# Masked attention and gated MLP on one core: who scales the first batch's probabilities, and when a table is cleared

## The chip, the cores and the metric

The kernel runs on one core of a Trainium2 chip, in one launch. The metric is device time in microseconds (us) of a whole execution. The engines of the core are named as the profile names them: PE (TensorE, matmuls; its weight loads are listed apart as PEld), DVE (VectorE), ACT (ScalarE), POOL (GpSimd) and SP (SyncE, whose queue issues all the DMAs of this kernel).

## The reference

Attention over 4 batches, 8 heads, 768 positions and head size 64, in which a query keeps only the first four keys (the sinks) and the last 128 keys up to itself (the window). The heads' outputs, side by side, go through an MLP with a width-3 convolution and a gate.

```python
scores = scale * np.matmul(q, k.transpose(0, 1, 3, 2))
keep = is_sink | in_window
scores = np.where(keep, scores, -1000000000.0)
a = np.exp(scores - np.max(scores, axis=-1, keepdims=True))
a = a / (np.sum(a, axis=-1, keepdims=True) + 1e-09)
attn = np.matmul(a, v)
...
h = np.maximum(x @ w_in, 0.0)            # 512 -> 1024
conv_out = sum(conv_w[k] * hp[:, k:k + S, :] for k in range(3))
gate = 1.0 / (1.0 + np.exp(-conv_out))
out = (h * gate) @ w_out                 # 1024 -> 512
```

The MLP weights arrive as float64, which the kernel reads as pairs of 32-bit words; the rest is float32.

## The kernel before, in words

**Attention.** Work is cut into pairs of heads (`g`, 16 of them, four to a batch) and query tiles of 128 rows (`t`, six to a pair), so a batch has 24 steps. `scores` multiplies a tile of queries with the keys of its window and of the sinks (L334 in the first batch, L337 and L338 later), for two heads into two PSUM tiles `sc`. DVE masks and takes the row's extreme (L498, L499), ACT takes the exponential in place in `pe` and sums it (L502), DVE adds and inverts the sums (L504, L505 into `sm`), and L507 multiplies `pe` by the inverse, one instruction per head, on POOL. One step later `transp` transposes `pe` on PE (L522), ACT copies it to `pT` (L524) and POOL cuts it at the diagonal (L526, L528). After three tiles `pv` multiplies with the values (L563) and with the sinks' values (L566), and ACT and DVE write the result as a high and a low part, `xH` and `xL` (L345, L346).

**Sink tables.** The first batch reads the sinks' values from `c.vs`, which lies in `room` (`roomH` in the profile): POOL clears it (L432), then six small DMAs fill it (L376). Later batches read `vsr`, a tile of its own in another format. It is zero but for small blocks that `sink_split` writes by DMA at the start of each later batch (L390). POOL also clears `A.zeros` in `room` (L430), from which other tiles are zeroed by DMA; `vsr` is one of them (L435).

**MLP.** `Moe.unit` makes 12 matmuls into `ph` (L183), the convolution and gate on ACT and DVE (L190 to L198), a high and a low part `g` on POOL (L200, L201), and matmuls into `po` (L210). These matmuls are the "fill" that is put between the attention steps. In the first batch only the first chunk's eight units can be filled in, in its second half, since they need attention results of all heads; from the second batch on there is fill for every step.

**Weights.** In the first batch the MLP weights are loaded in 16 pieces of 512 KB (L100), narrowed from 64 bits (ACT L111, DVE L112, L113, L114 on tiles named `stm` in the profile), rounded to a high part by ACT (L121) and a low part by POOL (L122). The `stm` tiles come from three buffers, so a new narrowing waits until POOL has read an old one.

**Order.** The code is written step by step, and a scheduler then orders each engine's instructions. Each engine and the SP queue run their own list in order.

Of the kernel before, what the change touches and what calls it, by code (L numbers as in the profile page):

```python
# [14 lines left out]
ALU = mybir.AluOpType  # L15
# [7 lines left out]
SR = 6 * NS  # L23
# [14 lines left out]
def f(ap):  # L38
    return ap.bitcast(F32)
# [323 lines left out]
def load_v(c, g, slot, lo=0, hi=None):  # L363
    hi = hi or c.S // P
    load(c, g, "v", c.v_raw[slot][:, lo:hi], lo, hi)
    return c.v_raw[slot]
# [12 lines left out]
def sink_split(c, m, vsr, b):  # L379

    raw, hi, lo = (m.mp.tile([P, 512], d, tag="st", name=f"sink{n}{b}", bufs=3)[0:NS] for d, n in ((F32, "r"), (F32R, "h"), (F32R, "l")))
    c.nc.sync.dma_start(raw.rearrange("s (h d) -> s h d", d=D), c.v[b].rearrange("h s d -> s h d")[0:NS])
    c.nc.scalar.copy(hi, raw)
    c.nc.vector.tensor_tensor(out=lo, in0=raw, in1=f(hi), op=ALU.subtract)
    for u in range(3):
        for part, val in enumerate((hi, hi, lo)):
            for j in range(2):
                r = SR * part + 2 * NS * u + NS * j
                dst, src = (f(x).rearrange("s (g j d) -> s g j d", j=2, d=D)[:, :, j] for x in (vsr[r:r + NS, u], val))
                c.nc.sync.dma_start(dst, src)  # L390


def banded(c):

    nc = c.nc
    m = Moe(c)
    A = Attn(c, m.x, KW, m.mp, m.ps)
    T = A.T
    NPAIR = c.H // 2
# [28 lines left out]
    n0, n1 = T * KW, 3 * NPAIR * P  # L428
# [2 lines left out]
    c.vs = m.room[0][0:6 * SP, n0:n0 + n1].rearrange("p (u n) -> p u n", u=3)  # L431
    nc.gpsimd.memset(c.vs, 0.0)  # L432
    vsr = cp.tile([3 * SR, 3, NPAIR * P], F32R, name="vsr")
    for h in range(2):
        nc.sync.dma_start(f(vsr).rearrange("p u n -> p (u n)")[:, n1 // 2 * h:n1 // 2 * (h + 1)], A.zeros[0:3 * SR, 0:n1 // 2])  # L435

    sms = [cp.tile([P, 10], F32, name=f"sm{i}") for i in range(5)]
    for sm in sms:
# [29 lines left out]
    def fetch(upto=len(queue)):  # L468

        while free[0] and asked[0] < min(len(queue), upto):  # L470
            free[0] -= 1
            g, nm, half = queue[asked[0]]
            st[g].raw[nm, half] = load_half(c, g, nm, half, c.raw[asked[0] % RAWB])
            asked[0] += 1
# [3 lines left out]
    def scores(g, t):  # L478
        s = st[g]
        lo = 0 if t == 0 else (t - 1) * KW  # L480
        mk = m0 if t == 0 else (m1 if t == 1 else m2)
        cols = slice(NS if t == 0 else 0, KW)
        sm = sms[A.tiles % len(sms)]
        A.tiles += 1
        hf, u = divmod(t, 3)
        if u == 0:
            s.pe[hf] = ap.tile([P, 3, 2, KW], F32, tag="pe", name=f"pe{g}_{hf}")
            if t == 0:
                nc.gpsimd.memset(s.pe[hf][:, 0, :, 0:NS], 0.0)
        pe = s.pe[hf][:, u]  # L490
        pcs = [ps.tile([P, SW], F32, tag="sc", name=f"sc{g}_{t}_{j}", bufs=2) for j in range(2)]
        if t == 0:
            A.scores(s, t, [pc[:, KW:SW] for pc in pcs], lo, lo + P)
        else:
            A.scores(s, t, pcs, lo, lo + SW)
        for j, pc in enumerate(pcs):
            if t:
                nc.vector.copy_predicated(pc[:, KW:SW], before.bitcast(I32), pc[:, 0:P])  # L498
            nc.vector.tensor_tensor_reduce(out=pe[:, j, cols], in0=pc[:, P:SW][:, cols], in1=mk, op0=ALU.add, op1=ALU.min,  # L499
                                           scale=1.0, scalar=3.0e38, accum_out=sm[:, j:j + 1])  # L500
        for j in range(2):
            nc.scalar.activation(pe[:, j, cols], pe[:, j, cols], AF.Exp, bias=sm[:, j:j + 1], scale=-1.0,  # L502
                                 accum_out=sm[:, 2 + 2 * j:3 + 2 * j])
        nc.vector.tensor_reduce(out=sm[:, 6:8], in_=sm[:, 2:6].rearrange("p (j e) -> p j e", e=2), op=ALU.add, axis=mybir.AxisListType.X)  # L504
        nc.vector.reciprocal(sm[:, 8:10], sm[:, 6:8])  # L505
        for j in range(2):
            nc.gpsimd.tensor_scalar(pe[:, j, cols], pe[:, j, cols], sm[:, 8 + j:9 + j], 1.0, ALU.mult, ALU.mult)  # L507

    def keytile(g, kt, hf):

# [37 lines left out]
    def pv(g, t):  # L548

        s = st[g]  # L550
        hp = g % NPAIR
        hf, u = divmod(t, 3)
        if u < 2:
            return
        px = ps.tile([P, 3, P], F32, tag="px", name=f"px{g}_{hf}").rearrange("p t k -> p (t k)")
        first = 3 * hf
        tiles = range(first + 2, max(0, first - 1) - 1, -1)
        for kt in tiles:
            pT = s.pT.pop((kt, hf)).rearrange("p h a k -> p h (a k)")
            lo, hi = max(kt, first), min(kt + 1, first + 2)  # L560
            cols = slice(P * (lo - kt), P * (hi - kt) + P)
            for j in range(2):
                nc.tensor.matmul(px[D * j:D * j + D, P * (lo - first):P * (hi - first) + P], s.v[:, kt, j, :], pT[:, j, cols],  # L563
                                 start=(kt == tiles[0]), stop=False, skip_group_check=True)
        for w in range(1 - hf, 3):
            nc.tensor.matmul(px[:, P * w:P * w + P], (vsr if g >= NPAIR else c.vs)[:, w, P * hp:P * hp + P], s.sT, start=False, stop=(w == 2),  # L566
                             skip_group_check=True)
        A.xout(g, hf, px)
# [3 lines left out]
    def prep(n):  # L572

        g, half = jobs[n]
        if g >= NPAIR and half:
            return []
        if g >= PLAIN:
            return A.prep(g, st[g], ahead)
        if half == 0 and g % 2 == 0:
            kks.append(f(ap.tile([P, 4, T, KW], F32R, tag="kk", name=f"kk{g}")))  # L580
        out = []
        for h in (half, half + 1)[0:1 + g // NPAIR]:
            out += A.prep32(g, h, st[g], kks[g // 2][:, g % 2], "po" if g < NPAIR and h == 0 else "h", ahead)
        return out

    def values(n):
        g, half = jobs[n]
        if g < NPAIR:
            st[g].v = load_v(c, g, n % 2, *((2, T) if half else (0, 3)))
        elif half == 0:  # L590
            st[g].v = load_v(c, g, g % 2)

    def coming(n):

        last = 2 * NPAIR - 2
        if n < last:
            return [(n + 1, -0.4, 1.8)]
        if n == last:
            return [(n + 1, -0.4, 1.4), (n + 2, 1.4, 5.6)]
        return [(n + 2, -0.4, 5.1)] if n % 2 == 0 and n + 2 < len(jobs) else []  # L600
# [10 lines left out]
    NSTB = NPAIR * T  # L611
# [8 lines left out]
    for i in range(NST + D2):  # L620
        if i < NST:
            n, g, t = steps[i]
            if t % 3 == 0:
                for n1, lo, hi in coming(n):
                    new = prep(n1)
                    todo += [(i + lo + (hi - lo) * (k + 1) / len(new), x) for k, x in enumerate(new)]
            if g >= NPAIR or t % 3 == 2:
                fetch()
            if t == 0 and g and g % NPAIR == 0:
                after = i + 3 if g > NPAIR else i  # L630
            if i == after:
                sink_split(c, m, vsr, g // NPAIR)
            if n + 1 < len(jobs) and (t % 3 == 2 if n < 2 * NPAIR else t == 3):
                values(n + 1)
        m.need(min(sum(i >= w for w in WHEN), len(m.todo)))
        for slot in range(SLOTS):
            if slot == 0 and i < NST:
                scores(g, t)
            if slot == 1 and 0 <= i - D1 < NST:
                transp(*steps[i - D1][1:])  # L640
            if slot == 2 and 0 <= i - D2 < NST:
                pv(*steps[i - D2][1:])
                if i - D2 + 1 in cuts:
                    while fill:
                        fill.pop(0)()
                    lo, hi, span = cuts[i - D2 + 1]
                    fill = m.pieces(lo, hi)
                    rate = len(fill) / (span - 0.5)
                    acc = 0.0
            acc += rate / SLOTS  # L650
            while acc >= 1.0 and fill:
                fill.pop(0)()
                acc -= 1.0
            while todo and i + (slot + 1) / SLOTS >= todo[0][0]:
                todo.pop(0)[1]()
# [73 lines left out]
def attention_gated_mlp(ctx: ExitStack, tc: tile.TileContext, q, k, v, n_sink, window, w_in, conv_w, w_out, out):  # L729
# [33 lines left out]
    with tc.If(fast == 1) as cmp:  # L763
        with ExitStack() as es:
            c.es = es
            banded(c)
# [32 lines left out]
```

## Time and profile before

| what | value |
|---|---|
| median of three runs | 490.69 us (490.53 to 490.93) |
| the profiled execution: its time | 490.92 us |
| the profiled execution: its span, first to last instruction | 489.2 us |
| busy: PE / PEld | 454.3 us (93%) / 386.4 us (79%) |
| busy: DVE / ACT / POOL | 344.4 us (70%) / 340.6 us (70%) / 325.5 us (67%) |
| share of the chain that ended last | PE 73%, POOL 11%, DVE 5%, ACT 4%, DMA 2% |
| mean granted TensorE clock | 0.999 |

Busy shares are averages over the whole span. The chain is read back from the last instruction, each time to what released it. So they do not say in which stretch an engine is short.

### The profile page before, as it was taken

The page shows a single profiled execution, that of the slowest core. Times are in us where ns is not written, and L with a number is a line of the kernel's source. Part 1 is how long each engine was busy: PE and PEld are TensorE (multiplying, and loading weights), DVE is VectorE, ACT ScalarE, POOL GpSimd, SP SyncE. Part 2 cuts the span into 40 slices and gives each one's busy share as a digit, 9 for nine tenths or more (in the row PEclk, how much of TensorE's full clock was granted, in tenths as well). Part 3 has the DMA queues.
Part 4 walks back from the last instruction along what each step waited for, and adds up shares of the span by engine and source line. Part 5 has one row for each costly group of instructions (what it writes and reads, how often), then busy time and mean ns, then how long its engine had stood idle before and what let it go on. Part 6 is the DMA issues. An engine that isn't in the chain of part 4 may idle for free.

```text
span 489.2 us, 10476 instructions
## 1 busy us (share of the span) xinstructions
PE 454.3 (93%) x3149; PEld 386.4 (79%) x3149; DVE 344.4 (70%) x1203; ACT 340.6 (70%) x1087; POOL 325.5 (67%) x622
## 2 busy tenths in 40 slices
PE   2878778899999999999999999999999999999993
PEld 1545566688788888888888888888889888999982
DVE  4697989857968786876677777776675664655551
ACT  3897868778767968886777877776776664545541
POOL 3489899976866877784867676685664564434341
PEclk9999999999999999999999999999999999999999
DMA  5788562537234241244141422223110100101001
GB/s 147 202 231 219 170 173 76 122 78 184 67 81 113 65 115 38 65 113 98 42 108 45 108 67 66 55 70 90 46 43 22 45 2 1 44 1 44 23 23 51
DMA packets 87306, 41.02 MB, mean 84 GB/s; under 512 B 80160, under 2 KB 80184, under 8 KB 87240
## 3 DMA queue, kind: packets, MB, share of 16 engines
q1 hardware_dynamic: 87240, 40.25, 31.7%
q8 instruction: 28, 0.46, 0.4%
q14 instruction: 38, 0.31, 0.2%
HBM read 27.60 MB, written 6.29 MB: 69 GB/s over the span
## 4 chain that ended last, share of the span: by engine, by line
PE 73%; POOL 11%; DVE 5%; ACT 4%; DMA 2%; issue 2%; SPq 1%; POOLq 0%; ACTq 0%; DVEq 0%
PE ph L183 26%; PE po L210 25%; PE px L563 7%; PE sc L337 3%; PE pts L522 3%; PE sc L338 3%; POOL pe L507 3%; PE tq L271 2%; PE px L566 2%; POOL wiL L122 2%; POOL pT L526 1%; ACT pe L502 1%; PE tk L289 1%; POOL woL L122 1%; POOL nq L263 1%
## 5 line engine op out<-in xcount | busy, mean ns | idle before, releaser
L210 PE MATMUL po<-woH,g 128*128 128x512 f32 x384 | 142.2, 408 | 5.1 <-POOL g L200 4.9
L183 PE MATMUL ph<-xH,wiH 128*128 128x258 f32 (+1 forms) x384 | 112.3, 292 | 1.1 <-ACT sT L538 0.9
L183 PE MATMUL ph<-xL,wiH 128*128 128x258 f32 (+1 forms) x384 | 109.0, 284 | 0.0
L183 PE MATMUL ph<-xH,wiL 128*128 128x258 f32 (+1 forms) x384 | 109.0, 284 | 0.0
L507 POOL TENSOR_SCALAR pe<-pe,sm 128x132 f32<-128x132 f32 (+1 forms) x192 | 85.0, 453 | 35.5 <-DVE sm L505 25.0
L195 DVE SCALAR_TENSOR_TENSOR t<-hb,cw,t 128x256 f32<-128x256 f32 x96 | 57.5, 600 | 42.7 <-ACT t L194 42.1
L502 ACT ACTIVATE pe<-pe,sm 128x132 f32<-128x132 f32 (+1 forms) x192 | 77.5, 406 | 14.4 <-DVE sm L499 13.8
L200 POOL TENSOR_SCALAR g<-t 128x256 fp32r<-128x256 f32 x96 | 41.6, 434 | 63.3 <-DVE t L198 47.8
L210 PEld LDWEIGHTS po<-woH,g 128*128 128x128 f32 x384 | 68.9, 189 | 16.9 <-POOL g L200 6.5
L201 POOL TENSOR_TENSOR g<-t,g 128x256 fp32r<-128x256 f32 x96 | 75.6, 788 | 5.7
L183 PEld LDWEIGHTS ph<-xH,wiH 128*128 128x128 f32 x384 | 72.7, 189 | 5.5 <-ACT sT L538 1.5
L210 PE MATMUL po<-woL,g 128*128 128x512 f32 x192 | 76.0, 396 | 0.0
L183 PEld LDWEIGHTS ph<-xH,wiL 128*128 128x128 f32 x384 | 72.7, 189 | 2.3
L183 PEld LDWEIGHTS ph<-xL,wiH 128*128 128x128 f32 x384 | 72.6, 189 | 0.7
L197 ACT ACTIVATE t<-t 128x256 f32<-128x256 f32 x96 | 40.0, 418 | 33.3 <-DVE t L196 32.6
L198 DVE SCALAR_TENSOR_TENSOR t<-t,hb 128x256 f32<-128x256 f32 x96 | 48.8, 509 | 16.7 <-ACT t L197 15.9
L499 DVE CUSTOM_DVE_ANT_0 pe<-sc,m 128x132 f32<-128x132 f32 (+1 forms) x192 | 53.3, 287 | 10.2 <-PE sc L338 8.5
L498 DVE COPY_PREDICATED sc<-before,sc 128x128 f32<-128x128 int32 x160 | 45.0, 289 | 18.5 <-PE sc L338 14.4
L196 DVE SCALAR_TENSOR_TENSOR t<-hb,cw,t 128x256 f32<-128x256 f32 x96 | 54.4, 567 | 4.3
L526 POOL TENSOR_SCALAR_AFFINE_SELECT pT<-pT 128x256 f32<-128x256 f32 x80 | 38.9, 487 | 27.0 <-ACT pT L524 26.5
L190 ACT ACTIVATE hb<-ph 128x258 f32<-128x258 f32 (+1 forms) x96 | 36.9, 385 | 27.9 <-PE ph L183 27.5
L194 ACT ACTIVATE t<-hb,cw 128x256 f32<-128x256 f32 x96 | 49.3, 513 | 8.4 <-POOL g L201 4.6
(123 smaller groups left out, 923.1 us busy)
## 6 DMA issues: line engine op xcount, KB each, us to landing
raw<-in_q_dram SPq DMA_DIRECT2D x64, 96.0 KB
raw<-in_k_dram SPq DMA_DIRECT2D x64, 96.0 KB
out_dram<-stm SPq DMA_DIRECT2D x24, 256.0 KB
kk<-kk SPq DMA_DIRECT2D x24, 198.0 KB
vraw<-in_v_dram SPq DMA_DIRECT2D x24, 192.0 KB
wi_0r<-in_moe_w_in_dram SPq DMA_DIRECT2D x2, 512.0 KB
wi_1r<-in_moe_w_in_dram SPq DMA_DIRECT2D x2, 512.0 KB
wi_2r<-in_moe_w_in_dram SPq DMA_DIRECT2D x2, 512.0 KB
```

The lines of the kernel that those rows point to most:

```text
L183: nc.tensor.matmul(u.h[:, 0:W], w[:, cc, ff * P:(ff + 1) * P], x[:, cc, t0:t1], start=(i == 0), stop=(i == len(prods) - 1))
L194: nc.scalar.mul(a, prev, cw[:, 0, ff:ff + 1])
L195: nc.vector.scalar_tensor_tensor(out=e, in0=this, scalar=cw[:, 1, ff:ff + 1], in1=a, op0=ALU.mult, op1=ALU.add)
L196: nc.vector.scalar_tensor_tensor(out=a, in0=nxt, scalar=cw[:, 2, ff:ff + 1], in1=e, op0=ALU.mult, op1=ALU.add)
L198: nc.vector.scalar_tensor_tensor(out=a, in0=e, scalar=1.0, in1=this, op0=ALU.add, op1=ALU.mult)
L201: nc.gpsimd.tensor_tensor(out=u.g[:, 1], in0=a, in1=f(u.g[:, 0]), op=ALU.subtract)
L210: nc.tensor.matmul(po[:, 0:c.DM], u.g[:, a, tt * P:(tt + 1) * P], w[:, ff, :], start=(ff == 0 and i == 0), stop=(ff == NFF - 1 and i == 2))
L498: nc.vector.copy_predicated(pc[:, KW:SW], before.bitcast(I32), pc[:, 0:P])
L499: nc.vector.tensor_tensor_reduce(out=pe[:, j, cols], in0=pc[:, P:SW][:, cols], in1=mk, op0=ALU.add, op1=ALU.min, scale=1.0, scalar=3.0e38, ...
L502: nc.scalar.activation(pe[:, j, cols], pe[:, j, cols], AF.Exp, bias=sm[:, j:j + 1], scale=-1.0, accum_out=sm[:, 2 + 2 * j:3 + 2 * j])
L507: nc.gpsimd.tensor_scalar(pe[:, j, cols], pe[:, j, cols], sm[:, 8 + j:9 + j], 1.0, ALU.mult, ALU.mult)
L526: nc.gpsimd.affine_select(out=keytile(g, t - 1, hf)[:, :, 1], in_=own, pattern=[[0, 2], [-1, P]], compare_op=ALU.is_gt, fill=c.zero, base= ...
```

## The change

Three places of `banded` are touched. In `scores`, the two multiplications of a step go to DVE for the pairs of the first batch (`g < NPAIR`: 24 steps, 48 instructions) and stay on POOL for the others. The two DMAs that zero `vsr` become a function, `clear`, which is called at step 12 of the first batch's 24 and no longer before the first step.

```diff
-    for h in range(2):
-        nc.sync.dma_start(f(vsr).rearrange("p u n -> p (u n)")[:, n1 // 2 * h:n1 // 2 * (h + 1)], A.zeros[0:3 * SR, 0:n1 // 2])
+    def clear():
+        w = vsr.shape[1] * vsr.shape[2] // 2
+        for h in range(2):
+            nc.sync.dma_start(f(vsr).rearrange("p u n -> p (u n)")[:, w * h:w * h + w], A.zeros[0:3 * SR, 0:w])
...
         for j in range(2):
-            nc.gpsimd.tensor_scalar(pe[:, j, cols], pe[:, j, cols], sm[:, 8 + j:9 + j], 1.0, ALU.mult, ALU.mult)
+            if g < NPAIR:
+                nc.vector.tensor_scalar(pe[:, j, cols], pe[:, j, cols], sm[:, 8 + j:9 + j], None, ALU.mult)
+            else:
+                nc.gpsimd.tensor_scalar(pe[:, j, cols], pe[:, j, cols], sm[:, 8 + j:9 + j], 1.0, ALU.mult, ALU.mult)
...
+        if i == NSTB // 2:
+            clear()
```

What the scheduler makes of it is seen in the built programs. First the SP queue near the program's start, before the change (`raw` are queries and keys, `wi` and `wo` weights, `vraw` values):

```order
8 L100 DMA wi_0r<-in_moe_w_in_dram 128x1024
9 L354 DMA raw_69<-in_q_dram 128x3x64 x2
10 L354 DMA raw_70<-in_k_dram 128x3x64
11 L435 DMA vsr<-roomH 72x768 x2
12 L376 DMA roomH<-in_v_dram 4x4x64 x6
13 L354 DMA raw_70<-in_k_dram 128x3x64
14 L100 DMA wi_1r<-in_moe_w_in_dram 128x1024
15 L354 DMA raw_67<-in_q_dram 128x3x64 x2
```

The same place of the SP queue with the change, up to where the clearing now stands (L438):

```order
9 L354 DMA raw_69<-in_q_dram 128x3x64 x2
10 L354 DMA raw_70<-in_k_dram 128x3x64 x2
11 L100 DMA wi_1r<-in_moe_w_in_dram 128x1024
12 L354 DMA raw_67<-in_q_dram 128x3x64
13 L376 DMA roomH<-in_v_dram 4x4x64 x6
...
24 L354 DMA raw_69<-in_q_dram 128x3x64 x2
25 L354 DMA raw_70<-in_k_dram 128x3x64 x2
26 L438 DMA vsr<-roomH 72x768 x2
27 L100 DMA wo0r<-in_moe_w_out_dram 128x1024
28 L354 DMA vraw_71<-in_v_dram 128x3x64 x2
```

The second weight piece `wi_1r` and the keys `raw_70` now stand ahead of the sink loads, and the clearing stands between the loads of the fourth pair's queries and keys and the first `wo` piece.

On POOL, the first instructions after the set-up, before the change:

```order
29 L122 TENSOR_TENSOR wiL<-stm_259,wiH 128x512
30 L507 TENSOR_SCALAR pe_0_208<-pe_0_208,sm_161 128x128 x2
31 L507 TENSOR_SCALAR pe_0_208<-pe_0_208,sm_162 128x132 x2
32 L507 TENSOR_SCALAR pe_0_208<-pe_0_208,sm_163 128x132 x2
33 L526 AFFINE_SELECT pT_0_0_245<-pT_1_0_283 128x2x128
```

and with the change on DVE, for the first tile, where the multiplication (now L512) stands among that engine's masks (L502, L503) and narrowing (L112, L113):

```order
33 L509 RECIPROCAL sm_159<-sm_159 128x2
34 L503 ISA pe_0_206,sm_160<-sc_1_0_227,m_134 128x132
35 L503 ISA sm_160 128x1
36 L512 TENSOR_SCALAR pe_0_206<-pe_0_206,sm_159 128x128 x2
37 L502 COPY_PREDICATED sc_1_1_228<-before,sc_1_1_228 128x128
38 L112 TENSOR_SCALAR stm_286<-stm_287 128x512
```

The 48 multiplications have left POOL's list and stand in DVE's, one to three instructions behind their reciprocal. From the second batch on the lists of all engines end alike (the last 5,388 of PE's 7,951 instructions, for one).

## Rows read from the trace of the kernel before

**Rows 1.** Busy time of each engine by stretch of the span, with a header.

```profile
core 0: us, PE busy (x) PEld busy (x) DVE busy (x) ACT busy (x) POOL busy (x), PEclk, DMA share, GB/s
9.50:30.30 20.80, 16.52 (x83) 11.72 (x83) 15.64 (x82) 17.46 (x61) 10.48 (x31) 1.00 0.84 217
30.30:94.50 64.20, 50.72 (x321) 37.78 (x319) 58.67 (x180) 51.24 (x159) 62.02 (x82) 1.00 0.59 163
94.50:130.00 35.50, 34.67 (x260) 29.62 (x261) 25.66 (x112) 27.68 (x98) 26.87 (x58) 1.00 0.43 106
130.00:480.00 350.00, 349.25 (x2479) 305.10 (x2477) 240.28 (x819) 240.87 (x766) 221.46 (x437) 1.00 0.23 59
```

**Rows 2.** The chain that ended last, 30.3 to 94.5 us, shares by line.

```profile
by line: POOL pe L507 16.8%; POOL wiL L122 12.6%; POOL pT L526 9.3%; POOL woL L122 9.1%; POOL pT L528 6.0%; POOL g L201 5.7%; POOL nq L263 5.5%; DVE stm L113 5.4%; issue 5.3%; DVE stm L114 4.7%; POOL g L200 4.1%; DMA raw<-in_q_dram 3.5%; DV
```

**Rows 3.** The same chain near the start: start us, us, what.

```profile
8.03 1.47 POOL roomH L432
...
9.55 0.75 SPq L435
...
13.36 4.88 DMA wi_1r<-in_moe_w_in_dram
```

**Rows 4.** Timeline of SP's queue: the two clearing DMAs.

```profile
8.55 1.75 SPq L435 DMA_DIRECT2D vsr<-roomH  x2
```

**Rows 5.** DMA issues by size: the same two.

```profile
vsr<-roomH SPq DMA_DIRECT2D x2, 216.0 KB
```

**Rows 6.** Timeline of ACT: where it sat idle after 15 us.

```profile
15.37 0.40 ACT L502 ACTIVATE pe<-pe,sm 128x132 f32<-128x132 f32 x1 [0.88 <-DVE sm L499]
...
17.14 0.49 ACT L250 ACTIVATE kk<-trk 128x384 f32<-128x384 f32 x1 [0.52 <-PE trk L313]
18.27 0.67 ACT L111 ACTIVATE stm<-wi_1r 128x512 f32<-128x512 f32 x1 [0.64 <-DMA wi_1r<-in_moe_w_in_dram]
```

**Rows 7.** Stretches, L507 alone: length, POOL busy (count), clock, DMA share, GB/s.

```profile
9.50:30.30 20.80, 5.96 (x14) 1.00 0.84 217
30.30:94.50 64.20, 16.09 (x28) 1.00 0.59 163
```

**Rows 8.** Timeline of DVE at 10.3 us: the same operation on masks, three in line.

```profile
10.37 0.49 DVE L426 TENSOR_SCALAR m<-m 128x128 f32<-128x128 f32 x3
```

**Rows 9.** DVE groups from 30 to 95 us: busy us, mean ns, idle before.

```profile
L114 DVE SCALAR_TENSOR_TENSOR stm<-stm,stm 128x512 int32<-128x512 int32 x13 | 11.9, 917 | 0.1
...
L112 DVE TENSOR_SCALAR stm<-stm 128x512 int32<-128x512 int32 x12 | 6.1, 508 | 4.2 <-POOL woL L122 2.4 <-POOL wiL L122 1.7
L198 DVE SCALAR_TENSOR_TENSOR t<-t,hb 128x256 f32<-128x256 f32 x5 | 4.8, 982 | 0.0
...
L195 DVE SCALAR_TENSOR_TENSOR t<-hb,cw,t 128x256 f32<-128x256 f32 x6 | 3.9, 667 | 0.0
```

**Rows 10.** The same for 160 to 440 us.

```profile
L195 DVE SCALAR_TENSOR_TENSOR t<-hb,cw,t 128x256 f32<-128x256 f32 x66 | 37.8, 572 | 24.9 <-ACT t L194 24.5
...
L198 DVE SCALAR_TENSOR_TENSOR t<-t,hb 128x256 f32<-128x256 f32 x65 | 31.6, 486 | 10.6 <-ACT t L197 10.1
```

**Rows 11.** Single lines of DVE: min/median/max ns (L195, L198 from 160 us).

```profile
L195 DVE SCALAR_TENSOR_TENSOR t<-hb,cw,t x66: 466/487/1066, 160.6 to 438.5; 128x256 f32<-128x256 f32 x66
...
L198 DVE SCALAR_TENSOR_TENSOR t<-t,hb x65: 404/425/1028, 163.5 to 437.5; 128x256 f32<-128x256 f32 x65
...
L112 DVE TENSOR_SCALAR stm<-stm x17: 265/417/1004, 11.2 to 81.6; 128x512 int32<-128x512 int32 x16, 24x128 int32<-24x128 int32 x1
```

**Rows 12.** Timeline of DVE at 12.4 us: L114 while POOL is idle.

```profile
12.36 0.69 DVE L114 SCALAR_TENSOR_TENSOR stm<-stm,stm 128x512 int32<-128x512 int32 x1
```

**Rows 13.** Waits of DVE from 30 to 95 us: total, times, longest.

```profile
DVE stm L112 <- POOL woL L122: 2.4, 1, 2.4
DVE stm L112 <- POOL wiL L122: 1.7, 1, 1.7
```

## The prediction, made before the changed kernel had run

> **What bounds the kernel now.** I first cut the span into stretches and read each engine's busy time [rows 1]. From 94.5 us on PE is the bound: it is busy 34.67 of 35.5 us and then 349.25 of 350. Both kernels give PE the same matmuls, so whatever moves the end of the first batch moves the end of the kernel by as much. Before 94.5 us PE is not the bound: from 30.3 to 94.5 us it is busy 50.72 of 64.2 us, while POOL is busy 62.02 (97%), DVE 58.67 (91%) and ACT 51.24. The second view, the chain that ended last in that stretch [rows 2], agrees: its large parts are POOL's, and L507, the line that is moved, is the largest at 16.8%. DVE's narrowing (L113, L114) has about 10% of it, so DVE stands close behind. The third view is the same chain near the start [rows 3]: POOL's clearing of `room`, then SP's queue (L435 and the sink loads behind it), then a 4.88 us wait for the weight piece `wi_1r`, issued at 13.36 us, after which ACT carries the chain to 30.3 us.
>
> So there are two questions: how much earlier can the crowded stretch begin, and how long does it last when DVE does part of POOL's work.
>
> **The clearing of `vsr`.** Its two issues hold SP's queue for 1.75 us from 8.55 us on [rows 4]. With the change they are gone from there, and by the program's order `wi_1r` even stands ahead of the six sink loads, so it goes out some 4 us earlier than 13.36. What that buys is bounded by ACT, which then has a full list until 30.3 us. ACT sat idle three times between 15 and 18.3 us [rows 6]: 0.88 us for DVE's mask, 0.52 us for the transposes of keys whose load stood behind the clearing, 0.64 us for `wi_1r`. The last two depend on the queue. I take **1.2 us**, their sum rounded; the ends are 0 and 2.0 us (all three). DVE has room for its extra work here: 14 of the 48 multiplications [rows 7] at the 0.23 us worked out below are 3.2 us, and DVE is idle 5.2 of 20.8 us [rows 1].
>
> The clearing itself is not gone. The order puts it behind the loads of the fourth pair, ahead of the `wo` pieces, well before the middle of the batch. It is two DMAs of 216 KB [rows 5]; at the 217 GB/s of that stretch they take 432/217 = 2.0 us of DMA time, while the DMA engines are 84% busy [rows 1]. I cost it at nothing, because by then ACT, DVE and POOL hold queued work and the `wo` pieces are loaded ahead of use; if that cover fails, the price is up to 2.0 us and the first term turns into a loss of 0.8.
>
> **POOL without the multiplications.** In the crowded stretch 28 of them take 16.09 us [rows 7], so POOL falls from 62.02 to 45.9 of 64.2 us, from 97% to 72%. It stops being the bound.
>
> **DVE with them.** No row shows this instruction on DVE. The nearest is the same operation on a mask tile of the same size: three in 0.49 us, one 0.22 us long, so (0.49 - 0.22)/2 = 0.137 us apart [rows 8]. That is the low end. It was taken with POOL calm. The same operation on larger tiles, L112, has a median of 417 ns but a mean of 508 in the crowded stretch [rows 9, 11], 0.09 us more. I take 0.137 + 0.09 = **0.23 us**, hence 28 x 0.23 = **6.4 us** more on DVE (3.8 at the low end).
>
> DVE also gets something back. Its instructions with two inputs in SBUF are stretched where POOL is busy: L114 takes 917 ns on average and 690 when POOL is idle; L198 takes 982 and L195 667 against medians of 425 and 487 later on [rows 9, 11, 12]. Summed over their counts, with L112, the excess is 13 x 0.23 + 5 x 0.56 + 6 x 0.18 + 12 x 0.09 = 8.0 us. Later, where POOL is busy 221 of 350 us (63%), the excess of L195 and L198 is 0.085 and 0.061 us [rows 10, 11], together a fifth of what it is here. POOL going from 97% to 72% is three quarters of the way to 63%, so I let three quarters of that four-fifths fall away: 0.6 x 8.0 = **4.8 us**. The ends are 2.1 (in proportion to POOL's busy time, 26%) and 6.4 us (all four-fifths).
>
> DVE then has 58.7 + 6.4 - 4.8 = 60.3 us to do. Of the 5.5 us that it is idle, 4.1 are waits for POOL to free `stm` tiles [rows 13]; these go when POOL is no longer late, and 1.4 stay. The stretch becomes 61.7 us instead of 64.2: **2.5 us** less, with DVE as the new bound at 98%. The last six multiplications fall behind 94.5 us, where DVE is idle 10 of 35.5 us [rows 1], and cost nothing unless PE should wait there.
>
> Behind the moved instruction stand the next masks and narrowing on DVE; PE's score matmuls wait for the masks, ACT and POOL for the narrowing. Ahead of it nothing new is waited for, since its reciprocal runs on the same engine.
>
> **Sum.** -1.2 - 2.5 = -3.7 us. Against the profiled execution's own 490.92 us (489.2 us of span and 1.7 around it) that is 487.2; against the median of 490.69, **487.0 us**.
>
> **Rivals.**
> *DVE blocked (slower).* Each moved instruction may have to wait for POOL's instruction under way instead of paying 0.09. With half of a POOL instruction of the kind that L507 is now, 16.09/28/2 = 0.29 us [rows 7], the price is 0.42, 28 of them 11.9 us; with the small relief of 2.1 DVE has 58.7 + 11.9 - 2.1 + 1.4 = 69.9 us, 5.7 more than now, less 1.2 at the start: 495.2 us. It decides from a price of 0.36 us up, where 58.7 + 28p - 4.8 + 1.4 reaches 64.2 + 1.2. For it speaks that single instructions of L112 took up to 1004 ns; against it that their median is 417 [rows 11]. The Trainium skill's page "SBUF — State Buffer", section "Who interferes with whom", says that VectorE in its two-port modes and GpSimd lock one pair of ports against each other for a whole instruction, and names `tensor_scalar` among those that take it. By that rule the moved work still holds the pair, and this rival would be the likeliest; the stretched means of L114 and L198 agree with the rule, L112's median does not.
>
> *Given back (no change).* DVE gets its 60.3 us, but the 5.5 us of idleness stay, because ACT, PE or the clearing's DMAs take POOL's place as what it waits for: 65.8 us, 1.6 more than now, less 1.2: 491.1 us. For it speaks that ACT and PE are busy 80% and 79% here [rows 1], against it that DVE's waits from 30 to 95 us are nearly all for POOL [rows 13].
>
> *The two engines come free of each other (much faster).* At 0.137 us a piece and with 6.4 us of relief DVE has 58.7 + 3.8 - 6.4 + 1.4 = 57.5 us: -6.7 - 1.2 = -7.9, 482.8 us. For it speaks the later stretch, where both engines run with little excess [rows 10]; against it that the weight pieces, the longest instructions of both, exist only in the first batch.
>
> **How the numbers follow.** Forecast 0.47 (485 to 489.7 on its own), much faster 0.20, no change 0.17 (taken as within 0.2%, about 1 us, the least that can be told from no change), blocked 0.16. Hence faster 0.67, same 0.17, slower 0.16. The range goes from the much faster case, 482.6, to the edge of the no-change case, 491.7; the blocked case lies outside.
>
> **What would show it.** In the profile of the changed kernel: `wi_1r` issued near 9 us and no idle ACT before its narrowing; POOL near 75% busy in the crowded stretch; the multiplication on DVE with a mean near 0.25 to 0.3 us (lengths overlap, so they exceed the spacing); L114 and L198 shorter on average; DVE above 95%; the first batch's last sink matmuls (L566 on `roomH`) some 3 to 4 us earlier than now; and everything behind them as long as before. I am wrong if the multiplication averages above 0.4 us, if DVE waits for ACT or loads in place of POOL, or if PE has new gaps behind the first batch.

## The result and the profile after

The changed kernel takes **494.91 us** (median of 4 runs, 493.99 to 495.61) against 490.81 for the kernel before beside it: ratio 1.008, 95% interval 1.0068 to 1.0092. I had forecast 487.0, so both sign and size are wrong. It is slower by 4.1 us, between the case "given back" (491.1) and the case "DVE blocked" (495.2).

The stretches come first, the same cuts as [rows 1].

```profile
core 0: us, PE busy (x) PEld busy (x) DVE busy (x) ACT busy (x) POOL busy (x), PEclk, DMA share, GB/s
9.50:30.30 20.80, 16.23 (x79) 10.75 (x79) 17.35 (x86) 17.24 (x59) 6.89 (x19) 1.00 0.82 215
30.30:94.50 64.20, 52.13 (x307) 39.91 (x307) 62.17 (x199) 46.98 (x144) 41.48 (x50) 0.92 0.57 157
94.50:130.00 35.50, 33.55 (x242) 27.37 (x241) 27.45 (x117) 28.98 (x102) 21.85 (x46) 1.00 0.49 119
130.00:480.00 350.00, 349.63 (x2493) 305.62 (x2492) 243.98 (x835) 242.60 (x776) 226.16 (x444) 1.00 0.23 59
```

POOL is relieved as expected (62.02 to 41.48 us) and DVE is the bound (62.17 of 64.2, 97%). But PE did fewer matmuls in the crowded stretch, 307 against 321, and its granted clock there is 0.92 where it was 1.00. From 130 us on PE is the bound as before (349.63 of 350 us, 349.25 before). The last six sink matmuls of the first batch start at 115.22 us; before they started at 110.25. Those 5.0 us are the longer span (493.9 against 489.2) but for 0.3 us.

Next are DVE's groups from 30 to 95 us, as in [rows 9]: busy us, mean ns, idle before. The last line is L196 in the kernel before.

```profile
L114 DVE SCALAR_TENSOR_TENSOR stm<-stm,stm 128x512 int32<-128x512 int32 x13 | 11.3, 870 | 0.0
L512 DVE TENSOR_SCALAR pe<-pe,sm 128x132 f32<-128x132 f32 x28 | 9.6, 383 | 0.0
...
L112 DVE TENSOR_SCALAR stm<-stm 128x512 int32<-128x512 int32 x12 | 6.5, 539 | 0.4 <-ACT stm L111 0.3
L196 DVE SCALAR_TENSOR_TENSOR t<-hb,cw,t 128x256 f32<-128x256 f32 x5 | 5.0, 1005 | 0.0
L195 DVE SCALAR_TENSOR_TENSOR t<-hb,cw,t 128x256 f32<-128x256 f32 x5 | 3.4, 673 | 0.0
...
L198 DVE SCALAR_TENSOR_TENSOR t<-t,hb 128x256 f32<-128x256 f32 x5 | 2.3, 457 | 0.2 <-ACT t L197 0.2
```

```profile
L196 DVE SCALAR_TENSOR_TENSOR t<-hb,cw,t 128x256 f32<-128x256 f32 x6 | 4.3, 714 | 0.1
```

The multiplication is L512 now. The waits for POOL of [rows 13] are gone, and nothing like them came in their place. What did not come in full is the relief. L198 is shorter as forecast, 457 ns in place of 982, and gives back 2.6 us; L114 went only from 917 to 870 ns. But L112 rose from 508 to 539, L195 from 667 to 673, and L196, which the prediction did not count, from 714 to 1005. Within 30.3 to 94.5 us the multiplications hold DVE for 10.07 us in place of 6.4, so 52.10 us are left for the rest of its work, of which it did 58.67 us in the same time before. The difference, 6.6 us, slid behind 94.5 us.

The timeline of the changed kernel shows where the long multiplications come from.

```profile
28.75 1.27 POOL L122 TENSOR_TENSOR wiL<-stm,wiH 128x512 fp32r<-128x512 f32 x1 [0.97 <-ACT wiH L121]
...
28.85 1.45 DVE L512 TENSOR_SCALAR pe<-pe,sm 128x132 f32<-128x132 f32 x2
...
33.22 1.27 POOL L122 TENSOR_TENSOR wiL<-stm,wiH 128x512 fp32r<-128x512 f32 x1
...
33.37 1.19 DVE L112 TENSOR_SCALAR stm<-stm 24x128 int32<-24x128 int32 x1
...
39.84 1.42 POOL L122 TENSOR_TENSOR woL<-stm,woH 128x512 fp32r<-128x512 f32 x1
...
40.25 1.29 DVE L512 TENSOR_SCALAR pe<-pe,sm 128x128 f32<-128x128 f32 x2
```

Each time DVE's row (`x2` is two multiplications in line) starts inside POOL's L122 and ends 0.07 to 0.28 us after it: 30.30 after 30.02, 34.56 after 34.49, 41.54 after 41.26. A 24x128 piece takes 1.19 us that way, though it is a small part of a 128x512 one. This is the behaviour that the Trainium skill's page "SBUF — State Buffer", section "Who interferes with whom", states as an exclusive lock that is held for the whole instruction; these rows agree with it.

Last, the granted clock. Before, it stood at 1.00 in the whole first batch. After, it falls to 0.50 (1.2 GHz) twice, in about 47 to 54 us and 81 to 84 us; here is the first time (columns as above).

```profile
42.00:46.00 4.00, 1.87 (x11) 1.23 (x9) 3.97 (x17) 2.74 (x9) 0.92 (x1) 1.00 0.85 224
46.00:48.00 2.00, 0.29 (x1) 0.18 (x1) 2.00 (x5) 0.85 (x3) 1.93 (x4) 0.71 0.79 225
48.00:52.00 4.00, 4.00 (x14) 3.24 (x14) 3.78 (x16) 2.94 (x11) 2.57 (x3) 0.50 0.12 43
52.00:54.00 2.00, 2.00 (x10) 1.51 (x11) 1.17 (x4) 1.75 (x6) 0.57 (x1) 0.58 0.64 147
```

PE was busy 2.16 of the 6 us from 42 to 48; its longest wait, 2.07 us, was for L512 on DVE, which was full. Then it worked without a gap, but at half the clock.

### The profile page after: what moved, and what is told of

Read it like the earlier page. It is cut to its first block, busy times and chain, and to the rows that moved or that the text cites. A ratio compares the mean times of both kernels' runs of the same rounds, so it can differ in the third digit from the quotient of the medians.

```text
span 493.9 us, 10472 instructions
## 1 busy us (share of the span) xinstructions
PE 459.3 (93%) x3149; PEld 389.3 (79%) x3149; DVE 357.8 (72%) x1251; ACT 340.8 (69%) x1087; POOL 302.2 (61%) x574
## 4 chain that ended last, share of the span: by engine, by line
PE 76%; DVE 12%; DMA 3%; ACT 3%; issue 2%; POOL 1%; SPq 1%; DVEq 0%; ACTq 0%; POOLq 0%
PE ph L183 26%; PE po L210 25%; PE px L570 8%; PE pts L529 3%; PE sc L337 3%; PE sc L338 3%; PE px L573 2%; PE tq L271 2%; DVE stm L113 2%; PE sc L334 2%; DVE stm L114 1%; PE tk L289 1%; DVE pe L512 1%; DVE sc L502 1%; DVE t L196 1%
## 5 line engine op out<-in xcount | busy, mean ns | idle before, releaser
L183 PE MATMUL ph<-xH,wiH 128*128 128x258 f32 (+1 forms) x384 | 112.4, 293 | 1.1 <-ACT kk L250 0.8
L183 PE MATMUL ph<-xH,wiL 128*128 128x258 f32 (+1 forms) x384 | 110.0, 286 | 0.0
L183 PE MATMUL ph<-xL,wiH 128*128 128x258 f32 (+1 forms) x384 | 109.4, 285 | 0.1
L195 DVE SCALAR_TENSOR_TENSOR t<-hb,cw,t 128x256 f32<-128x256 f32 x96 | 56.0, 583 | 35.4 <-ACT t L194 34.5
L514 POOL TENSOR_SCALAR pe<-pe,sm 128x132 f32<-128x132 f32 (+1 forms) x144 | 60.0, 428 | 32.1 <-DVE sm L509 24.2
L183 PEld LDWEIGHTS ph<-xH,wiH 128*128 128x128 f32 x384 | 73.2, 191 | 5.8 <-ACT kk L250 1.0
L201 POOL TENSOR_TENSOR g<-t,g 128x256 fp32r<-128x256 f32 x96 | 74.3, 774 | 5.5
L183 PEld LDWEIGHTS ph<-xH,wiL 128*128 128x128 f32 x384 | 73.1, 190 | 2.2
L183 PEld LDWEIGHTS ph<-xL,wiH 128*128 128x128 f32 x384 | 73.1, 190 | 1.1 <-DVE xL L346 0.3
L198 DVE SCALAR_TENSOR_TENSOR t<-t,hb 128x256 f32<-128x256 f32 x96 | 47.6, 496 | 19.5 <-ACT t L197 19.0
L503 DVE CUSTOM_DVE_ANT_0 pe<-sc,m 128x132 f32<-128x132 f32 (+1 forms) x192 | 53.0, 288 | 11.3 <-PE sc L338 9.0
L502 DVE COPY_PREDICATED sc<-before,sc 128x128 f32<-128x128 int32 x160 | 44.5, 290 | 22.6 <-PE sc L338 19.0
L196 DVE SCALAR_TENSOR_TENSOR t<-hb,cw,t 128x256 f32<-128x256 f32 x96 | 55.4, 577 | 4.5 <-DVE sm L508 0.4
L533 POOL TENSOR_SCALAR_AFFINE_SELECT pT<-pT 128x256 f32<-128x256 f32 x80 | 41.3, 517 | 27.3 <-ACT pT L531 26.9
```

What stands on the lines that cost most here:

```text
L183: nc.tensor.matmul(u.h[:, 0:W], w[:, cc, ff * P:(ff + 1) * P], x[:, cc, t0:t1], start=(i == 0), stop=(i == len(prods) - 1))
L195: nc.vector.scalar_tensor_tensor(out=e, in0=this, scalar=cw[:, 1, ff:ff + 1], in1=a, op0=ALU.mult, op1=ALU.add)
L196: nc.vector.scalar_tensor_tensor(out=a, in0=nxt, scalar=cw[:, 2, ff:ff + 1], in1=e, op0=ALU.mult, op1=ALU.add)
L198: nc.vector.scalar_tensor_tensor(out=a, in0=e, scalar=1.0, in1=this, op0=ALU.add, op1=ALU.mult)
L201: nc.gpsimd.tensor_tensor(out=u.g[:, 1], in0=a, in1=f(u.g[:, 0]), op=ALU.subtract)
L533: nc.gpsimd.affine_select(out=keytile(g, t - 1, hf)[:, :, 1], in_=own, pattern=[[0, 2], [-1, P]], compare_op=ALU.is_gt, fill=c.zero, base= ...
```

## The experiments

Four theories were open: the price of the multiplications on a full DVE; the clearing at its new place; the new order, since the scheduler rearranged every engine's list of the first batch; the clock that falls where PE waits. All ratios are against the kernel before on the same chip.

**One part at a time.** e1 has the multiplications on DVE and the clearing where it was, e2 the reverse.

```diff
+    clear()                      # e1: called at its old place, not at NSTB // 2
-            if g < NPAIR:        # e2: only the clearing is moved, POOL multiplies
-                nc.vector.tensor_scalar(pe[:, j, cols], ...)
```

> The multiplications go to DVE, the clearing of vsr stays at the start. Theory DVE-full (the moved multiplications fill DVE and the first batch waits for it): as slow as the change or a little slower, 494 to 496.5 us, with DVE at 96% or more from 30 us to the end of the first batch. Rival, the clearing (its DMAs and the new order of the loads cost the time): 490 to 491.5 us, since the clearing is where it was. Rival, the TensorE clock (gaps on PE bring the granted clock to 1.2 GHz and this costs the time): between 493 and 496 with stretches at 0.5 in the first batch, and no such time if the stretches are missing.

> Only the clearing of vsr is moved, POOL multiplies as before. Theory DVE-full: the clearing is no loss, and the start gives what the prediction's first term said: 489 to 490.5 us. Rival, the clearing: 493 us or more. Rival, the clock: no low stretch in the first batch, 489 to 491 us.

e1: 497.57 us, 1.015 (1.0136 to 1.0164). e2: 493.16 us, 1.0049 (1.0036 to 1.0063). Each part alone is slower, and they don't add up (6.9 and 2.5 against 4.1 together). Something goes with each edit that is neither of them. By e2 alone the clearing would be a loss, as its rival had it (493 us or more).

**Half the multiplications, and a PE kept busy.** e3 puts the first head's on DVE and leaves the second's on POOL. e4 is the changed kernel with four more transposes a step.

```diff
-            if g < NPAIR:
+            if g < NPAIR and j == 0:                           # e3
+        for j in range(4 if g < NPAIR else 0):                 # e4
+            nc.tensor.transpose(pt[:, j % 2, :], c.ident, c.ident)
```

> In the first batch the first head's multiplication goes to DVE and the second head's stays on POOL, the clearing is moved as in the change. Theory DVE-full: DVE gets half as much more, so it and POOL are both near 93% and the time falls between: 489 to 492 us. Rival, the clearing: 493 us or more as with the change. Rival, the clock: follows from whether low stretches are there.

> The change, with four extra transposes of the identity on PE ahead of each step's two transposes in the first batch (96 in all, about 0.11 us each, 10.6 us of PE work that no result needs; they are overwritten). Rival, the clock: the gaps on PE get shorter, no stretch at 1.2 GHz is left in the first batch, and the time falls to 491 to 493.5 us although PE does more. Theory DVE-full alone: the clock may be whole, but the time stays at 494.5 us or rises to 498.

e3: 495.31 us, 1.0102 (1.0087 to 1.0118), above the 489 to 492 us that I expected and no better than all of them on DVE. Its order is again one of its own. e4: 500.21 us, 1.0209 (1.0182 to 1.0237), with the same two falls of the clock: the extra work did not close the gaps, and PE was busy 9.5 us longer (468.8 against 459.3). e4 tells nothing on the clock.

**The order held fixed.** From here on each engine's list is pinned: the scheduled list of the kernel before (or of the changed one) is written into the kernel, and each instruction gets an edge without a semaphore to the one ahead of it. Only the instructions under test are free, so they alone move.

```diff
+    for seq in lists:            # one per engine, in the recorded order
+        for a, b in zip(seq, seq[1:]):
+            tc.add_manual_dep(ins[b], ins[a].name, NoSync)
```

> Every engine keeps the order of instructions of the kernel before, except that the first batch's 48 multiplications are taken from POOL's list and put into VectorE's behind their reciprocals; the clearing stays at its old place. If the new order made by the scheduler is what costs the time (theory A), this kernel shows what the multiplications alone do: between the 487 us forecast and 491.5, with a granted clock near 0.999. If a full VectorE is what costs it (theory B: 10 us more of its time in a stretch where it is busy 97%), the time is 494 us or more, as with e1's 497.6, whatever the order.

> The order of the kernel before on every engine; only the two DMAs that clear the sink table stand at their new place in SP's queue, behind the loads that they follow in the changed kernel. POOL multiplies. Theory A (order): no later than before, 489 to 491 us, since the loads ahead come up to 2 us earlier and no order changes. Theory C (the transfer's new place disturbs other loads or SP): about 493 us, as e2 with its own order.

> The order of the kernel before with both edits: the multiplications in VectorE's list, the clearing at its new place on SP. Theory A (order): 487 to 491.5 us, at a clock near 0.999. Theory B (VectorE full): 494 to 497 us, no better than the changed kernel's 494.9.

> The order of the changed kernel on every engine, with the clearing at its new place, but POOL does the first batch's multiplications as before. Theory A (order): as slow as the changed kernel or slower, 494 to 497 us, with stretches at 1.2 GHz in the first batch. Theory B (VectorE full): 10 us of work are taken off VectorE, so the time falls back to 490 to 493 us.

| first batch multiplied by | order of the kernel before | order of the changed kernel |
| --- | --- | --- |
| POOL | e6: 490.78 us, 0.9993 (0.998 to 1.0005) | e8: 496.78 us, 1.0109 (1.0088 to 1.013) |
| DVE | e7: 498.60 us, 1.0139 (1.0113 to 1.0165) | changed kernel: 494.91 us, 1.008 |

e5, as e7 with the clearing at its old place, took 498.97 us, 1.0153 (1.0127 to 1.018). So the clearing at its new place does nothing in the old order, and e2's 2.5 us were its order. The multiplications cost 7.8 us in the old order (e7 against e6), where theory A wanted no loss. But e8 came out where theory A wanted it, 494 to 497 us, and theory B, a full DVE, wanted 490 to 493. With POOL's multiplications the new order costs 6.0 us (e8 against e6), and with DVE's it gives back about 3 of the 7.8. Neither theory holds alone: the two edits' effects do not add, and the 4.1 us of the change cannot be split into a share of the order and a share of the multiplications.

DVE's total and its L112 from 30 to 97 us, in e6 and then in e7, show where they go.

```profile
PE 454.6 (93%) x3149; PEld 386.7 (79%) x3149; DVE 343.7 (70%) x1203; ACT 340.7 (70%) x1087; POOL 326.1 (67%) x622
...
L112 DVE TENSOR_SCALAR stm<-stm 128x512 int32<-128x512 int32 (+1 forms) x13 | 5.8, 445 | 4.9 <-POOL wiL L122 1.7 <-ACT stm L111 1.7 <-POOL woL L122 1.4
```

```profile
PE 462.1 (93%) x3149; PEld 392.4 (79%) x3149; DVE 360.5 (72%) x1251; ACT 340.7 (68%) x1087; POOL 298.3 (60%) x574
...
L512 DVE TENSOR_SCALAR pe<-pe,sm 128x132 f32<-128x132 f32 (+1 forms) x30 | 12.0, 438 | 0.0
...
L112 DVE TENSOR_SCALAR stm<-stm 128x512 int32<-128x512 int32 (+1 forms) x14 | 10.1, 720 | 0.7 <-ACT stm L111 0.5
```

Over the program 48 multiplications with a mean length of 0.41 us put 17.7 us on DVE (neighbours overlap) in place of the 11 that 0.23 us apiece would be, and its busy time grows by 16.8: the relief of everything else is 0.9 us. It is the remainder of larger parts. In lengths over the program L198 and L114 are 3.9 us shorter, the relief as I had meant it, while L112 and L113 are 6.3 us longer. DVE's 4.9 us of waiting ahead of L112, 3.1 of it for POOL, fell to 0.7 from 30 to 97 us, and L112 itself took 4.3 us more.

**The multiplications on neither engine, and L122 off POOL.**

```diff
-            nc.gpsimd.tensor_scalar(pe[:, j, cols], ...)       # e9: not for g < NPAIR
-        nc.gpsimd.tensor_tensor(out=L, in0=w, in1=f(H), op=ALU.subtract)
+        nc.scalar.copy(L, w)                                   # e10, e11
```

> The kernel of e6 (order of the kernel before, clearing at its new place) with the first batch's 48 multiplications left out on both engines, so its output lacks that scaling. It shows what the removal from POOL alone gives. The prediction's terms (relief of VectorE 4.8 us, and VectorE's 4.1 us of waits for POOL gone) would make it about 482 to 484 us. If the relief is small and the waits turn into something else, it is 487 to 490 us. The difference to e7's 498.6 is the price of the multiplications on VectorE alone.

> The kernel of e7 (order of the kernel before, both edits), with the 16 subtractions of L122, POOL's longest instructions of the first batch, replaced by plain copies on ScalarE; the low halves of the split weights are then not the reference's. Theory L (VectorE's instructions stand still while POOL's subtraction runs): the multiplication falls from a mean of 0.41 to about 0.29 us, L112 from 0.67 to about 0.42, VectorE's busy time by 8 to 10 us, and the time from 498.6 to 489 to 493 us. Theory N (48 more instructions on a full engine, each slow by itself): the multiplication stays near 0.4 us and the time above 495.

> The kernel of e6, where POOL multiplies, with the same replacement of L122 by copies on ScalarE (low halves not the reference's): what e10 is to be set beside. Theory L: L112 and L114 take less time too, POOL is relieved by some 15 us, and the time is 484 to 489 us; the distance to e10 is then what the multiplications cost on VectorE without the subtractions beside them, 2 to 5 us in place of the 7.8 between e6 and e7. Theory N: the distance stays at 7 to 8 us.

e9: 490.21 us, 0.9992 (0.9972 to 1.0011). Without the multiplications on any engine, the kernel is no faster. POOL has 25 us less to do and DVE's busy time rises to 347.0 us, 3.3 more than in e6. Its timeline tells why (two of four such places):

```profile
46.19 1.27 POOL L122 TENSOR_TENSOR woL<-stm,woH 128x512 fp32r<-128x512 f32 x1 [0.47 <-ACT woH L121]
46.24 1.51 DVE L112 TENSOR_SCALAR stm<-stm 128x512 int32<-128x512 int32 x1
...
53.95 1.28 POOL L122 TENSOR_TENSOR wiL<-stm,wiH 128x512 fp32r<-128x512 f32 x1 [2.01 <-ACT wiH L121]
54.13 1.38 DVE L112 TENSOR_SCALAR stm<-stm 128x512 int32<-128x512 int32 x1
```

A POOL that is free starts L122 as soon as ACT's rounding ends, next to DVE's narrowing of the next piece; from 30 to 97 us L112 takes 9.8 us in place of 5.8. In e6 a late POOL ran such an L122 while DVE stood idle for its buffer:

```profile
41.20 1.28 POOL L122 TENSOR_TENSOR woL<-stm,woH 128x512 fp32r<-128x512 f32 x1
42.54 0.57 DVE L112 TENSOR_SCALAR stm<-stm 128x512 int32<-128x512 int32 x1 [1.38 <-POOL woL L122]
```

e10: 488.44 us, 0.9947 (0.9934 to 0.996). e11: 485.41 us, 0.9885 (0.9871 to 0.99). Both leave the subtraction out. With it gone from POOL the multiplications cost 3.0 us on DVE, not 7.8. And e11 takes as much work off POOL as e9 (POOL is busy 302.6 and 301.4 us) and is 4.8 us faster: what counts is which instructions leave POOL, not how much of its time. In e10, from 30 to 97 us:

```profile
L512 DVE TENSOR_SCALAR pe<-pe,sm 128x132 f32<-128x132 f32 (+1 forms) x34 | 11.1, 367 | 0.1
...
L112 DVE TENSOR_SCALAR stm<-stm 128x512 int32<-128x512 int32 (+1 forms) x13 | 5.8, 447 | 2.6 <-ACT stm L111 2.5
```

L112 is back at 447 ns (720 in e7), near its median of 417 [rows 11]; theory L holds. DVE's busy time fell by 14.3 us where I expected 8 to 10. The multiplication fell less than expected, to a mean of 0.345 us over the program where 0.29 was expected, since POOL's other instructions are still there: its two longest, of 1.04 us, lie inside or across L263. Theory N had the distance between e10 and e11 stay at 7 to 8 us, and is out.

**Can it be used?** e12 gives one head's multiplications to ACT. e13 has POOL multiply and DVE subtract, and e14 every second subtraction on DVE; these three leave nothing out.

```diff
+            if g < NPAIR and j: nc.scalar.mul(pe[:, j, cols], pe[:, j, cols], sm[:, 8 + j:9 + j])   # e12
-        nc.gpsimd.tensor_tensor(out=L, in0=w, in1=f(H), op=ALU.subtract)
+        nc.vector.tensor_tensor(out=L, in0=w, in1=f(H), op=ALU.subtract)                            # e13
```

> The kernel of e6 with the multiplication of one of the two heads moved from POOL to ScalarE, which is busy 52.5 us of 67 in the first batch's crowded stretch (POOL 64.3, VectorE 60.1). 24 multiplications, 16 in the stretch, by 0.3 to 0.45 us are 5 to 7 us more for ScalarE and as much less for POOL. If POOL's load is what the stretch waits for, 487 to 489.5 us; if the stretch waits for VectorE and the low clock, 490 to 493.

> The kernel of e6 (order of the kernel before, clearing at its new place, POOL multiplies) with all 16 subtractions of L122 done by VectorE in place of POOL; nothing is left out. By L346's 128x384 at 544 ns a 128x512 subtraction would take about 0.72 us, so 11.5 us more for VectorE; e11 shows 6.4 us less of its time when POOL's subtractions are gone. Theory L (collisions are the cost): VectorE's busy time grows by about 5 us in sum, POOL falls by 20 us, the time is 486 to 491. Rival (VectorE's count of work decides): busy time up by 11 us or more, and 494 us or more as in e7.

> As e13, with every second of the 16 subtractions on VectorE and the others left on POOL. Theory L: half of the collisions go, half of the subtractions come: VectorE's busy time grows by 2 to 3 us, POOL's falls by 10 us; 487 to 491 us. Rival: 492 us or more.

e12: 492.38 us, 1.0026 (1.0016 to 1.0036): relieving POOL by 13 us does not pay, as in e9, though here ACT got 5.3 us more. e13: **487.52 us**, 0.994 (0.992 to 0.9961), faster than both kernels. e14: 489.55 us, 0.998 (0.9971 to 0.9988), about half way in time, but not in DVE's busy time: that rose by 5.3 us (349.0 against 343.7) where I expected 2 to 3, and e13 with twice the subtractions adds only 4.5. The page of e13, and its DVE groups from 9 to 135 us:

```profile
PE 455.6 (94%) x3149; PEld 387.0 (80%) x3149; DVE 348.2 (72%) x1219; ACT 339.6 (70%) x1087; POOL 307.5 (63%) x606
...
L112 DVE TENSOR_SCALAR stm<-stm 128x512 int32<-128x512 int32 (+1 forms) x17 | 7.2, 425 | 2.5 <-ACT stm L111 2.4
...
L122 DVE TENSOR_TENSOR woL<-stm,woH 128x512 fp32r<-128x512 f32 x8 | 6.3, 793 | 0.2 <-ACT woH L121 0.2
L122 DVE TENSOR_TENSOR wiL<-stm,wiH 128x512 fp32r<-128x512 f32 x8 | 6.2, 778 | 0.3 <-ACT wiH L121 0.3
```

DVE got 12.5 us of subtractions and is busy only 4.5 us longer than in e6, so the rest of its work took 8 us less. e11, with the subtractions on neither engine, shows 6.4 us less (337.3 against 343.7). Its last sink matmuls of the first batch start at 107.03 us, 3.1 earlier than e6's 110.11. The rival, that DVE's count of work decides, wanted 494 us or more.

## Why the prediction was wrong, point by point

**"DVE also gets something back", 4.8 us: the step that failed.** I took DVE's excess to fall with POOL's busy share. In the same order the net relief was 0.9 us (e7 against e6), and with the multiplications gone from both engines it was a loss of 3.3 (e9). L198 and L114 did get shorter; L112 and L113 got longer by more. What stretches DVE is the meeting with single long POOL instructions, L122 above all, and whether they meet is set by when they start. Where POOL was late, DVE was held by the buffer in idle time; where POOL is early, it is held inside its own instruction. For the same reason the 4.1 us of waits [rows 13] went away as forecast and gained nothing. e10, e11 and e13 show it by taking L122 away.

**"DVE with them", 0.23 us: mis-sized.** The term counts busy time, in which neighbours overlap. By that count L512 cost 10.07/30 = 0.34 us in the changed kernel's crowded stretch and 17.7/48 = 0.37 in e7. As lengths it has a median of 0.282 us, a mean of 0.383 from 30 to 95 us in the changed kernel and 0.438 from 30 to 97 in e7. I added L112's excess in the kernel before, 0.09 us. That sample was not fair: there L112 twice waited for L122 to end, because it needs the buffer that L122 reads [rows 13], and so did not meet it. Where POOL is early, as in e9, L112's own mean is 753 ns from 30 to 97 us. DVE's new instruction waits for no such buffer.

**The weighing of the rivals.** "DVE blocked" has the mechanism and a price (0.42) that is too high but nearer to the measured 0.34 to 0.37 than mine. I set L112's median against the Trainium skill's rule and gave it 0.16. Its 495.2 us is 0.3 from the median, and that is luck: it counts 1.2 us gained at the start, of which nothing is seen, and in the old order the price of the multiplications is 7.8 us, of which the scheduler's new order takes about 3 back. No part of the prediction considered the order.

**The clearing, -1.2 us: nothing of it is seen.** The cause is there: `wi_1r` was issued at 9.02 us, and ACT reads it at 14.83 without a gap, where it used to be 18.27 [rows 6]. (Between the idle times listed there lies a fourth, 0.26 us for DVE, which I left out; the term does not use it.)

```profile
9.02 0.48 SPq L100 DMA_DIRECT2D wi_1r<-in_moe_w_in_dram  x1
...
14.83 0.65 ACT L111 ACTIVATE stm<-wi_1r 128x512 f32<-128x512 f32 x1
```

But the first batch ends later all the same. e6 has the clearing moved in the old order, where the sink loads still stand ahead of `wi_1r`: it is issued at 11.98 us in place of 13.36, ACT reads it at 17.80, 0.5 us earlier, and waits 0.74 us in place of 0.52 for the transposes just before. e6 takes 490.78 us against 491.18, no difference that can be told. So no run shows what the early `wi_1r` of the changed kernel is worth by itself. That the clearing itself costs nothing at its new place was right, as far as e6 shows it.

**POOL from 97% to 72%** was right in kind: 41.48 of 64.2 us is 65%, with 50 instructions in the stretch where the removal alone leaves 54. That this is worth anything was wrong; e9 and e12 show that POOL's load did not set the time, although the chain gave it the largest shares [rows 2].

**"What moves the first batch's end moves the kernel's end"** held: 5.0 us at the last sink matmuls, 4.7 in the span. (The range's lower end, 482.6, should have been the 482.8 of its case; nothing hangs on that.)

**What stays open** is how much of the 4.1 us is the clock. The falls come behind PE's waits for DVE, and the 10 us at 1.2 GHz lie in the stretch where DVE is the bound, so I take it that PE would have waited for part of them anyway. Runs of one kernel differ: the changed kernel took 493.99 us at a mean clock of 0.993 and 495.40 to 495.61 at 0.982 to 0.986; e9 took 488.17 at 0.998 and 491.74 to 493.97 at 0.982 to 0.985, though also 491.80 at 0.991. More time at the low level goes with a longer run, by 1.5 us in the one and 3.6 to 5.8 in the other, but even the changed kernel's best run is 3 us above the kernel before. In e10 there is no such link: 488.23 us at 0.995 and 488.27 at 0.986. The 7.8 us between e6 and e7 hold a part of the clock too. Here are e6 and then e7 late in the first batch (columns as above):

```profile
96.40:103.20 6.80, 6.80 (x54) 5.24 (x52) 2.68 (x8) 4.44 (x14) 5.99 (x13) 1.00 0.30 66
96.40:103.20 6.80, 6.07 (x17) 4.73 (x18) 5.68 (x20) 4.95 (x18) 4.12 (x9) 0.51 0.28 59
```

PE is nearly full there at half the clock. e7's run with the highest mean clock, 0.989, took 495.72 us, which is still 4.9 above e6. No run here separates DVE's part from the clock's.

## What to carry to other kernels

Before moving work from POOL to DVE, list the long POOL instructions that run beside it in the timeline, and price each moved DVE instruction with the chance of meeting them, not by its own length or the median of its kin alone. A wait that vanishes is a gain only if what it waited out does not come back inside the next instruction. Where two engines hold each other up, moving the long instruction to the engine that is held up can pay (e13) even if that engine is the fuller one. And where a scheduler reorders everything around an edit, compare with the order held fixed before judging the edit.

## What the hardware did that I had not expected

DVE's instructions that read PSUM were not stretched by POOL: the mask L503 took 281 ns on average from 30 to 95 us, as L499 did before, and L346 539 against 544. The lines that were stretched work from SBUF to SBUF (L112, L113, L114, L195, L196, L198 before the change, L512), though not all such lines were: the reciprocal L509 took 153 ns against 155. I had priced POOL's pressure on DVE as one share of busy time.

The granted clock fell in this kernel while PE stood waiting, and at the low level the same matmul takes half as long again: L183 has a median of 419 ns from 50 to 53 us and 283 from 56 to 70. What a row of them costs is more than that, since they overlap: they start 0.21 us apart at the low level (51.58, 51.79, 52.01) and 0.12 at the full one (58.51, 58.63, 58.75).

```profile
L183 PE MATMUL ph<-xL,wiH x3: 416/419/419, 51.6 to 52.9; 128*128 128x258 f32 x3
...
L183 PE MATMUL ph<-xL,wiH x12: 277/283/388, 57.1 to 69.6; 128*128 128x258 f32 x12
```
